# Layer one's last two token chunks of the first gMLP half as seven block products instead of eight

## The chip, the cores and the metric

One core of a Trainium2 chip. The time is the device time of one execution in microseconds (us). The engines are named as in the profile: PE (matrix products), PEld (its weight loads), DVE, ACT, POOL (vector, activation and GpSimd engines) and SP (the queue that issues most DMAs). Each engine runs its own queue in order and waits on semaphores for the others.

## What is computed

Two layers, each a linear-attention block and a gMLP block, on 2048 tokens of 512 features:

```python
x = x + A(layernorm(x))        # q, k, v; kv = pk^T v; o = pq kv / (pq . z); o @ wo
x = x + B(layernorm(x))
def B(x):
    z = gelu(x @ w_in)                     # (2048, 1792)
    z1, z2 = z[:, :896], layernorm(z[:, 896:])
    g = w_sp @ z2 + b_sp                   # mixing over the 2048 tokens
    return (z1 * g) @ w_out
```

The change concerns `z1`, the first half of `gelu(x @ w_in)`, in the first of the two layers (L = 0 in the code).

## The kernel before, in words

All products run on PE in fp32r parts: each operand is split into a high part (a rounded copy, made by ACT, `high`) and a low part (the rest, made by DVE, `low`), and a product is three matrix instructions (high by high, high by low, low by high).

Tokens are handled in 16 tiles of 128, and in four chunks of 512 (four tiles). For each layer there are three stages: `P1` (keys, queries, and the sum over keys), `P2` (attention output, second layer norm, and `x @ w_in`), and `P4` (mixing and `w_out`). `P2.run` is layer one's version of the second stage, a loop over steps s = 1 to 18. In step s it does, for different tiles:

- `b_high`, `b_low`: the queries of tile s, which went through DRAM to be turned, are turned back by DVE and split (ACT, then DVE);
- `c`, `c2`, `c3`: the attention output of tile s-1 on PE (12 instructions of 512 columns), added to x and its statistics taken on DVE, three small steps on POOL (`rs`, `rs`, `nb`), and the normalised tile (ACT) stored to DRAM in turned form (`yt`);
- `d_high`, `d_low`: tile s-2, back from DRAM, turned by DVE, split by ACT and DVE into its quarter of the chunk operand `xT`;
- `e`, `e2`, `e3`: tile s-3 times the second half of `w_in` (24 instructions of 448 columns), gelu on ACT, statistics on DVE, the three small steps on POOL; `e4`, one step later, normalises it on ACT;
- `f`: outputs of the first half, one (chunk, block of 128 features) each: 12 instructions of 512 columns, gelu (ACT), stored to DRAM. There are 4 chunks by 7 blocks. A chunk's seven become possible when its fourth tile is done (`d_low` with k == 3), and each step takes up to two.

`sums` are sums of blocks of `w_sp` for the seven-product mixing: a `tick` loads blocks, POOL makes two sums, and SP stores them two at a time. Layer one's P2 makes a tick in each step, and four are left (`LEFT`) for the first steps of its mixing. The five `f` that are left after step 18 run at the start of `P4.run`, while the first weights of the mixing are split (`sp`) and the first sums of z are made (`zahead`).

Layer two (`run2`, and the generator `tail`) already computes chunks 2 and 3 by seven products: the chunks are the two halves of the tokens, the features of x are halved, and the blocks f and f+3 of the weights are the two halves of the outputs. Three triples of weight sums (`FSums`) are made in layer two's `P1` on POOL and kept in DRAM (`w1sums`). `first_a` and `first_b` are products of chunk 2 alone; `T1`, `T2`, `raw` make sums of the token halves on DVE; `tail` has products 5, 6, 7, 3 and 4 for the three block pairs. A `yield` in it lets `P4.run` split the mixing's first weights in between. The seventh block (f = 6) is computed plainly.

The order on each engine is that of the code: nothing is reordered afterwards.

Of the kernel before, what the change touches and what calls it, by code (L numbers as in the profile page):

```python
# [152 lines left out]
def mixer_kernel(ctx: ExitStack, tc: tile.TileContext, x_in, wqkv, wo_d, win1_d, win2_d, wsp_d, bsp_d, wout_d,  # L153
# [299 lines left out]
    class P1:  # L453
# [187 lines left out]
        def run(self, sums):  # L641
            side = deque([self.win2] * NF)
            ND = NT - DEFER
            for s in range(1, NT + 2):
# [54 lines left out]
                if self.L:  # L699
                    if 9 <= s < NT + 1:  # L700
                        sums.halve(28 + (s - 9) // 2, None, (s - 9) % 2)
                    if s in WADD:
                        if not WADD[s]:
                            self.fsums = FSums()
                        self.fsums.load(WADD[s])
                    if s - 1 in WADD:
                        self.fsums.sums(WADD[s - 1])
                    if s - 2 in WADD:
                        self.fsums.split(WADD[s - 2])
                        if WADD[s - 2] == 2:  # L710
                            self.fsums.close()
# [15 lines left out]
    class FSums:  # L727


        def __init__(self):  # L730
            self.raw = quads.get([P, 2, 2, 512])
            self.parts = quads.get([P, 2, 2, 512], F32R)

        def load(self, f):
            for k in range(2):
                nc.sync.dma_start(self.raw[:, f % 2, k], win1_d[f + 3 * k])

        def sums(self, f):
            p, q = (self.raw[:, f % 2, k].rearrange("p (k n) -> p k n", k=2) for k in range(2))
            for o, a, b, op in ((q[:, 1], q[:, 0], q[:, 1], OP.add), (q[:, 0], p[:, 0], q[:, 0], OP.subtract),  # L740
                                (p[:, 0], q[:, 1], p[:, 0], OP.subtract), (p[:, 1], p[:, 1], p[:, 0], OP.subtract)):
                nc.gpsimd.tensor_tensor(o, a, b, op=op)

        def split(self, f):
            p, q = (self.raw[:, f % 2, k].rearrange("p (k n) -> p k n", k=2) for k in range(2))
            for m in range(2):
                h, l = (self.parts[:, m, k] for k in range(2))
                for k, s in enumerate((q[:, 1 - m], p[:, m])):
                    high(h[:, 256 * k:256 * k + 256], s)
                for k, s in enumerate((q[:, 1 - m], p[:, m])):  # L750
                    low(l[:, 256 * k:256 * k + 256], s, h[:, 256 * k:256 * k + 256])
                for k in range(2):
                    nc.sync.dma_start(w1sums[f, m][k], self.parts[:, m, k].bitcast(F32))

        def close(self):
            quads.put(self.raw, self.parts)
# [72 lines left out]
    class P2:  # L829
        def __init__(self, p1):  # L830
            self.L = L = p1.L
            self.p1 = p1
            self.win1, self.win2 = None if L else w_in1(), p1.win2
            self.ws = deque()
            self.wf = deque([w1parts[f] for f in list(range(NF)) * 2 + [0, 6, 1, 2, 6]]
                            + [w1sums[f, m] for m in range(2) for f in range(3)]
                            + [[t[:, 256:512] for t in w1parts[f + 3]] for f in range(3)])
            self.draw, self.S, self.fdone, self.qhome, self.zacc, self.meant = {}, {}, None, {}, {}, set()
            self.qturn, self.xturn = Turn(f"qt{L}", range(5), True), Turn(f"yt{L}", (0, 1, 2, 3, NT - 1) if L else range(4), home=ZHome if L else None)
# [44 lines left out]
        def b_high(self, i):  # L884
            b, home = self.qturn.get(i)
            self.qhome[i] = ZHome(i) if self.L and i > FIRSTPAIR else pages
            h = self.qhome[i].get([P, 4, P], F32R)
            high(h, b)
            self.bpart = b, home, h
# [23 lines left out]
        def c3(self, i):  # L913
# [3 lines left out]
            own = self.L and i > FIRSTPAIR  # L917
# [25 lines left out]
        def d_low(self, i):  # L943
# [9 lines left out]
            if k == 3:  # L953
                self.fnext = [(n, f) for f in (range(NF) if n < 2 or not self.L else (NF - 1,))]
# [149 lines left out]
        def f(self, hold=False, home=pages):  # L1104
# [19 lines left out]
            if f == NF - 1 and not (self.L and n > 1):  # L1124
                quads.put(*self.xT.pop(n))
# [38 lines left out]
        def first_a(self, *fs):  # L1164

            A = nc.scalar.activation
            for f in fs:
                w = self.A[f] = self.ws.popleft()
# [5 lines left out]
        def first_b(self, *fs):  # L1174

            for f in fs:
                w = self.A[f]
                self.fmul(self.u[f], [t[:, 256:512] for t in w], [t[:, 2:4] for t in self.xT[2]], False, True)
                pages.put(*w)

        def first_out(self, *fs):
            for f in fs:
                if f:
                    self.wfetch()
# [26 lines left out]
        def tail(self):  # L1211
            V, A = nc.vector, nc.scalar.activation
            h, l = (t.bitcast(F32) for t in self.xT[3])
            big = [bigs.get([P, NF, 512], F32R if k < 2 else F32) for k in range(3)]
            c = [big[2][:, f] for f in range(3)]
            room = Rooms(big[2][:, f] for f in range(3, NF))
# [11 lines left out]
            self.p4.loadb()  # L1228
# [10 lines left out]
            for f in range(3):  # L1239
# [4 lines left out]
                if f == 0:  # L1244
                    self.e3m(NT - 2)
                    self.e3m(NT - 1)
                if f == 1:
# [6 lines left out]
            self.e3(NT - 2)  # L1254
            self.e3(NT - 1)
            self.e4(NT - 4)
            self.e4(NT - 3)
# [19 lines left out]
            for i in (NT - 2, NT - 1):  # L1277
                _, rs, nb = self.zms.pop(i)
                V.tensor_scalar(ztile[i], ztile[i], rs, nb, op0=OP.mult, op1=OP.add)
            for f in range(3):  # L1280
                w = self.ws.popleft()
                self.fmul(d[f], w, self.T[4], False, True)
                pages.put(*w)
# [4 lines left out]
            bigs.put(*big)  # L1288

        def run(self, sums):  # L1290
# [4 lines left out]
            for s in range(1, NT + 3):  # L1295
                if s == NT + 2:
                    sums.tick()
# [17 lines left out]
                else:  # L1315
# [29 lines left out]
                self.f()  # L1345
                self.f()
# [4 lines left out]
                if self.L == 0:  # L1351
                    if s > 4:
                        sums.tick(s < NT + 2)
# [4 lines left out]
                if s >= NT + 1:  # L1358
                    self.p4.fetch(s - NT - 1)
# [270 lines left out]
    class P4:  # L1630
# [622 lines left out]
        def run(self, nxt):  # L2253
            p2 = self.p2
            early = nxt is None
            if not early:
                self.fetch(3)
                self.sp(0)
                self.fetch(4)
            self.zmade = 0  # L2260
            if not early:
                self.zahead(1)
            n = 0
            if early:
                for _ in p2.tail():
                    n += 1
                    self.zahead(n - 1)
                    self.sp(n - 1)
                    if n < 3:
                        self.fetch(n + 3)  # L2270
                self.zahead(3)
            while p2.f():
                self.zahead(min(self.zmade, 3))
# [3 lines left out]
                if n == SPN:  # L2277
                    self.sp(1)
                    self.fetch(5)
            self.zahead(3)  # L2280
            if p2.win1 is not None:
                p2.win1.free()
# [4 lines left out]
            for g in range(n):  # L2287
# [11 lines left out]
                if not early and g == 14:  # L2299
                    self.sums.fetch()  # L2300
                if not early and 15 <= g <= 15 + LEFT:
# [117 lines left out]
```

## Time and profile before

| | |
|---|---|
| median of 3 runs | 1346.38 us (1345.5 to 1346.66) |
| the profiled execution | 1345.32 us |
| its span, first to last instruction | 1343.5 us |
| busy share: PE, DVE, ACT, POOL | 100%, 78%, 54%, 34% |

Lists of groups have the line, engine, operation, tiles written and read, count, busy time, mean length of one, and the idle time before them with what ended it. A timeline has start and length in us first. A matrix instruction's length in the profile is longer than its share of PE, since they overlap: what one costs is the time from its start to the start of the next. Layer one's P2 lies at 133 to 331 us of the span, and its mixing starts at 350.3 us.

### The profile page before, as it was taken

The numbers are of one execution on the slowest core, as the hardware profiler recorded it, in microseconds if no ns is written. First come the engines' busy times: TensorE is split into PE (matmuls) and PEld (weight loads), VectorE is DVE, ScalarE is ACT, GpSimd is POOL, SyncE is SP. The second block draws the span as 40 slices with busy tenths as digits, with TensorE's granted clock in tenths as the row PEclk, the third lists the DMA queues.
The fourth block names the chain that finished last, engine by engine and source line by source line (L and its number), as shares of the span: only waits on it lengthen the run. The fifth ranks groups of instructions, "written<-read, shape, count | busy, mean of one in ns | idle before, by whom it ended". The sixth has DMA issues, their size and how long they took to land.

```text
span 1343.5 us, 19219 instructions
## 1 busy us (share of the span) xinstructions
PE 1338.9 (100%) x6547; PEld 1142.0 (85%) x6547; DVE 1042.9 (78%) x1662; ACT 726.6 (54%) x1219; POOL 460.2 (34%) x613
## 2 busy tenths in 40 slices
PE   9999999999999999999999999999999999999999
PEld 7888888888888888889988888888888888888898
DVE  7779877753797699898867878777679858899885
ACT  5764634334642265445677755557687433666454
POOL 3755765534122400301425443544531012122021
PEclk9999999999999999999999999999999999999999
DMA  5898477878977986894777662678767545579344
GB/s 184 284 313 282 158 256 250 284 254 270 316 234 256 289 267 203 282 320 80 174 169 235 167 142 84 202 243 259 229 211 234 170 164 176 178 245 312 123 79 64
DMA packets 172403, 290.30 MB, mean 216 GB/s; under 512 B 14480, under 2 KB 53904, under 8 KB 172048
## 3 DMA queue, kind: packets, MB, share of 16 engines
q1 hardware_dynamic: 154048, 251.45, 56.5%
q0 software_dynamic: 18112, 37.49, 13.4%
q8 instruction: 51, 0.84, 0.3%
q14 instruction: 48, 0.39, 0.1%
q10 hardware_dynamic: 144, 0.13, 0.0%
HBM read 204.08 MB, written 101.71 MB: 228 GB/s over the span
## 4 chain that ended last, share of the span: by engine, by line
PE 98%; DVE 1%; DMA 0%; ACT 0%; POOL 0%; issue 0%; SPq 0%; POOLq 0%
PE bank L230 14%; PE bank L228 14%; PE bank L229 14%; PE bank L1922 12%; PE bank L1923 12%; PE bank L1924 12%; PE bank L2120 3%; PE bank L2121 3%; PE bank L2122 3%; PE bank L988 1%; PE bank L989 1%; PE bank L990 1%; PE bank L384 1%; PE bank L1155 1%; PE bank L1157 1%; PE bank L1156 1%
## 5 line engine op out<-in xcount | busy, mean ns | idle before, releaser
L1923 PE MATMUL bank<-qd,pg 128*128 128x512 f32 x736 | 286.4, 389 | 0.0
L1922 PE MATMUL bank<-qd,pg 128*128 128x512 f32 x736 | 286.3, 389 | 0.0
L1924 PE MATMUL bank<-qd,pg 128*128 128x512 f32 x736 | 286.3, 389 | 0.0
L1697 ACT ACTIVATE qd<-qd 128x1024 fp32r<-128x1024 f32 x142 | 149.5, 1053 | 128.2 <-PE bank L1924 108.0
L1700 DVE TENSOR_TENSOR qd<-qd,qd 128x1024 fp32r<-128x1024 f32 x132 | 167.8, 1274 | 54.1 <-ACT qd L1697 54.1
L230 PE MATMUL bank<-qd,pg 128*128 128x512 f32 x448 | 174.7, 390 | 0.0
L1924 PEld LDWEIGHTS bank<-qd,pg 128*128 128x128 f32 x736 | 138.2, 188 | 28.8
L1923 PEld LDWEIGHTS bank<-qd,pg 128*128 128x128 f32 x736 | 138.2, 188 | 28.6
L1922 PEld LDWEIGHTS bank<-qd,pg 128*128 128x128 f32 x736 | 138.2, 188 | 28.6
L1963 POOL TENSOR_TENSOR bg<-bg,pg 128x512 f32<-128x512 f32 x28 | 46.9, 1676 | 217.9 <-ACT qd L1697 100.3
L228 PE MATMUL bank<-qd,pg 128*128 128x512 f32 x308 | 120.2, 390 | 0.2 <-ACT pg L214 0.2
L229 PE MATMUL bank<-qd,pg 128*128 128x512 f32 x308 | 120.0, 390 | 0.0
L230 PEld LDWEIGHTS bank<-qd,pg 128*128 128x128 f32 x448 | 84.1, 188 | 18.2 <-DVE pg L217 0.4
L363 POOL TENSOR_SCALAR rs<-mv 128x1 f32<-128x1 f32 x80 | 24.7, 308 | 191.3 <-DVE mv L361 186.9
L214 ACT ACTIVATE pg<-pg 128x512 fp32r<-128x512 f32 x85 | 53.0, 624 | 64.6 <-DVE pg L448 21.3
L372 ACT ACTIVATE pg<-pg,nb,rs 128x512 f32<-128x512 f32 x52 | 42.1, 812 | 84.5 <-POOL nb L366 79.0
L1606 POOL TENSOR_TENSOR pg<-pg,pg 128x512 f32<-128x512 f32 x48 | 67.2, 1400 | 58.2 <-DVE pg L1762 52.1
L2122 PE MATMUL bank<-wo,qd 128*128 128x256 f32 x288 | 81.5, 283 | 0.0
L2120 PE MATMUL bank<-wo,qd 128*128 128x256 f32 x276 | 78.1, 283 | 0.0
L2121 PE MATMUL bank<-wo,qd 128*128 128x256 f32 x276 | 78.0, 283 | 0.0
L229 PEld LDWEIGHTS bank<-qd,pg 128*128 128x128 f32 x308 | 57.8, 188 | 12.1 <-DVE qd L217 0.3
L228 PEld LDWEIGHTS bank<-qd,pg 128*128 128x128 f32 x308 | 57.8, 188 | 12.1 <-ACT pg L214 0.4
(278 smaller groups left out, 3280.4 us busy)
## 6 DMA issues: line engine op xcount, KB each, us to landing
qd<-s SPq DMA_DIRECT2D x62, 512.0 KB, 4.4
qd<-in_wsp_dram SPq DMA_DIRECT2D x40, 512.0 KB, 4.1
qd<-hP SPq DMA_DIRECT2D x40, 512.0 KB, 4.7
pg<-z SPq DMA_DIRECT2D x56, 256.0 KB, 4.7
pg<-in_wsp_dram SPq DMA_DIRECT2D x52, 256.0 KB, 4.3
s<-pg SPq DMA_DIRECT2D x48, 256.0 KB, 3.8
z<-pg SPq DMA_DIRECT2D x40, 256.0 KB, 3.3
pg<-w POOLq DMA_DIRECT2D x38, 256.0 KB, 4.7
```

The lines of the kernel that those rows point to most:

```text
L228: nc.tensor.matmul(out, ah, bh, start=start, stop=False)
L229: nc.tensor.matmul(out, ah, bl, start=False, stop=False)
L230: nc.tensor.matmul(out, al, bh, start=False, stop=stop)
L1606: nc.gpsimd.tensor_tensor(t, a, b, op=OP.add)
L1697: self.mark = nc.scalar.activation(w[:, 0], r, AF.Copy)
L1700: nc.vector.tensor_sub(w[:, 1], r, w[:, 0].bitcast(F32))
L1922: m(out, h[:, o], w[:, 0, j, :], start=start, stop=False, skip_group_check=True)
L1923: m(out, h[:, o], w[:, 1, j, :], start=False, stop=False, skip_group_check=True)
L1924: m(out, l[:, o], w[:, 0, j, :], start=False, stop=stop, skip_group_check=True)
L2120: m(out, A, x, start=start and f == 0, stop=False, skip_group_check=True)
L2121: m(out, A, y, start=False, stop=False, skip_group_check=True)
L2122: m(out, B, x, start=False, stop=stop and f == 2, skip_group_check=True)
```

## The change

Layer one's P2 takes chunks 2 and 3 by the same seven products. The tables that set the order are changed, `tail` serves both layers, and the weight sums are made in layer one's steps 13 to 16, on DVE and ACT, and stored for layer two. The shares of the first token half (`m = 0`) are kept in memory until `tail` uses them, those of `m = 1` are loaded again from DRAM in step 18. The split weights of layer one are stored to DRAM five steps earlier (`WSTORE`). Ticks of block sums stop after step 13, and ten instead of four are made in the mixing, from its 14th step on. Normalised tiles and query parts are held in the z tiles instead of pages (`ZHome`). Layer two's P1 no longer makes the weight sums.

```diff
-WSTORE = 9
+WSTORE = 4
+FONE = {6: 2, 7: 2, 8: 2, 9: 1, 10: 2, 11: 2, 12: 2, 13: 1, 14: 1}
-WADD = {2: 0, 4: 1, 6: 2}
+WADD = {13: 0, 14: 1, 15: 2}
-LEFT = 4
+LEFT = 10
+TLAST = 13
+TFIRST = 13
...
         def split(self, f):
+            raw = self.raw.pop(f)
+            p, q = (t.rearrange("p (k n) -> p k n", k=2) for t in raw)
+            V = nc.vector
+            V.tensor_add(q[:, 1], q[:, 0], q[:, 1])
+            V.tensor_sub(q[:, 0], p[:, 0], q[:, 0])
+            V.tensor_sub(p[:, 0], q[:, 1], p[:, 0])
+            V.tensor_sub(p[:, 1], p[:, 1], p[:, 0])
             for m in range(2):
...
-                self.fnext = [(n, f) for f in (range(NF) if n < 2 or not self.L else (NF - 1,))]
+                self.fnext = [(n, f) for f in (range(NF) if n < 2 else (NF - 1,))]
...
+                if s in (15, 16, 17):
+                    self.first_a(s - 15)
+                if s == NT + 1:
+                    self.T1()
+                    self.T1split()
+                    self.raw(1)
+                    self.T2()
+                if s == NT + 2:
+                    self.ws.extend(self.fsums.kept)
+                    quads.put(*self.xT.pop(2))
+                    for _ in range(3):
+                        self.wfetch()
                 if s >= 4:
                     self.e4(s - 4)
...
                     self.e3(s - 3)
-                self.f()
-                self.f()
+                for _ in range(FONE.get(s, 0)):
+                    self.f()
+                if s in (15, 16, 17):
+                    self.first_b(s - 15)
+                    self.first_out(s - 15)
+                if s - 2 in WADD:
+                    self.fsums.store()
+                if s in WADD:
...
+                    self.fsums.load(WADD[s])
+                if s - 1 in WADD:
+                    self.fsums.split(WADD[s - 1])
+                if s == NT:
+                    self.B = quads.get([P, 2, 2, 512])
+                    self.raw(0)
...
-            while p2.f():
-                self.zahead(min(self.zmade, 3))
+            for _ in p2.tail():
```

Three places of the built program, where the steps above the mixing stand. Tiles are named by pool (`pg` pages, `qd` quads, `bg` bigs, `z_z` a tile of the second half) and a running number.

DVE in step 16 and at the head of step 17 before the change: the add of tile 15's attention output to x with its statistics, the turning and low part of tile 14, the statistics of z13, then the turning of tile 15.

```order
L909 TENSOR_TENSOR pg_339_3238<-pg_339_3238,bank_131_3492 128x512
L359 BN_STATS st<-pg_339_3238 128x6
L361 BN_AGGR mv<-st 128x2
L448 STREAM_TRANSPOSE pg_362_3520<-pg_355_3405 128x4x128
L217 TENSOR_TENSOR qd_17_3279<-pg_362_3520,qd_16_3278 128x4x128
L359 BN_STATS st<-z_z_3553 128x6 x2
L361 BN_AGGR mv<-st 128x2
L448 STREAM_TRANSPOSE pg_367_3606<-pg_363_3525 128x4x128
L217 TENSOR_TENSOR qd_17_3279<-pg_367_3606,qd_16_3278 128x4x128
```

The same piece now, from the statistics of z13 on: four sums of a pair of weight blocks, four low parts, and `raw(0)` stand ahead of tile 15's turning.

```order
L362 BN_STATS st<-z_z_3558 128x6 x2
L364 BN_AGGR mv<-st 128x2
L733 TENSOR_TENSOR pg_330_3470<-pg_330_3470 128x256
L734 TENSOR_TENSOR pg_330_3470<-pg_329_3468,pg_330_3470 128x256
L735 TENSOR_TENSOR pg_329_3468<-pg_330_3470,pg_329_3468 128x256
L736 TENSOR_TENSOR pg_329_3468<-pg_329_3468 128x256
L220 TENSOR_TENSOR pg_338_3590<-pg_330_3470,pg_337_3589 128x256
L220 TENSOR_TENSOR pg_338_3590<-pg_329_3468,pg_337_3589 128x256
...
L1160 TENSOR_TENSOR qd_18_3601<-qd_14_2766,qd_15_2767 128x1024
L451 STREAM_TRANSPOSE z_y<-pg_335_3530 128x4x128
L220 TENSOR_TENSOR qd_17_3281<-z_y,qd_16_3280 128x4x128
```

Steps 14 and 15 have such a block of eight at their ends too, where they had none.

DVE from tile 15's low part to the first operand of product 6 now (before, only the two statistics of z14 and z15 stood there): `T1`, its low part, `raw(1)`, the eight of `T2`, the two statistics, and the low part of product 6's operand, `bg_7`.

```order
L220 TENSOR_TENSOR qd_17_3281<-z_y,qd_16_3280 128x4x128
L1194 TENSOR_TENSOR qd_18_3601<-qd_16_3280,qd_18_3601 128x1024
L1195 TENSOR_TENSOR qd_18_3601<-qd_18_3601,qd_17_3281 128x1024
L220 TENSOR_TENSOR qd_19_3618<-qd_18_3601,qd_19_3618 128x1024
L1160 TENSOR_TENSOR qd_18_3601<-qd_14_2766,qd_15_2767 128x1024
...
L1211 TENSOR_TENSOR pg_342_3623<-pg_342_3623,qd_17_3281 128x512
L362 BN_STATS st<-z_z_3661 128x6 x2
...
L362 BN_STATS st<-z_z_3727 128x6 x2
L364 BN_AGGR mv<-st 128x2
L220 TENSOR_TENSOR bg_7_3744<-pg_343_3624,bg_7_3744 128x512
```

ACT over the same stretch now: the high part of `T1`, then z13 normalised, gelu of z14, an output's gelu, z14 normalised, gelu of z15, z15 normalised, and only then the high part of product 6's operand.

```order
L217 ACTIVATE qd_19_3618<-qd_18_3601 128x1024
L375 ACTIVATE z_z_3558<-z_z_3558,nb,rs 128x896
L1068 ACTIVATE z_z_3661<-bank_137_3635 128x448
L1143 ACTIVATE pg_345_3680<-bank_136_3608 128x512
L375 ACTIVATE z_z_3661<-z_z_3661,nb,rs 128x896
L1068 ACTIVATE z_z_3727<-bank_139_3701 128x448
L375 ACTIVATE z_z_3727<-z_z_3727,nb,rs 128x896
L217 ACTIVATE bg_7_3744<-pg_343_3624 128x512
```

Before, the same rows for z13 to z15 stood there, but what followed them was the split of the mixing's first weight, not an operand that the next product reads.

More of the change, by code (lines that the diff above doesn't have):

```diff
@@ L730, in __init__ @@
         def __init__(self):
[L731 to L732 removed]
+            self.raw, self.kept, self.made = {}, deque(), []
         def load(self, f):
[L735 to L742, printed above, removed]
[L744 to L745 removed]
+            self.raw[f] = [load(win1_d[f + 3 * k]) for k in range(2)]
+        def split(self, f):
+            raw = self.raw.pop(f)
[5 more added lines that the diff above has]
+            V.tensor_sub(p[:, 1], p[:, 1], p[:, 0])
             for m in range(2):
[L747 removed]
+                h, l = pages.get(PAGE, F32R), pages.get(PAGE, F32R)
                 for k, s in enumerate((q[:, 1 - m], p[:, m])):
@@ L1123, in f @@
                 self.wfetch()
-            if f == NF - 1 and not (self.L and n > 1):
+            if f == NF - 1 and n < 2:
                 quads.put(*self.xT.pop(n))
@@ L1288, in tail @@
             bigs.put(*big)
+            if not L:
+                pages.put(*c)
         def run(self, sums):
```

118 lines of the change are left out of this document (58 added, 60 removed).

## The prediction

> **What bounds the kernel now.** I read the page first: busy shares, then the chain that ended last.
>
> ```profile
> span 1343.5 us, 19219 instructions
> PE 1338.9 (100%) x6547; PEld 1142.0 (85%) x6547; DVE 1042.9 (78%) x1662; ACT 726.6 (54%) x1219; POOL 460.2 (34%) x613
> PE 98%; DVE 1%; DMA 0%; ACT 0%; POOL 0%; issue 0%; SPq 0%; POOLq 0%
> ```
>
> PE is busy throughout and is 98% of the chain. A product that goes therefore shortens the span, and anything that makes PE wait lengthens it at once: there is no other slack to take it up. What a product costs, and how near the other engines are, I read from the busy time by stretches, cut at the first matrix instruction of a step: steps 13, 14, 17, 18, then the five last outputs `f`.
>
> ```profile
> 269.25:279.59 10.34, 10.34 (x50) 9.02 (x48) 6.63 (x14) 2.95 (x6) 4.36 (x7) 1.00 0.77 259
> 279.59:292.64 13.05, 13.05 (x61) 11.27 (x60) 7.71 (x11) 4.83 (x8) 5.31 (x10) 1.00 0.84 271
> 318.75:326.36 7.61, 7.61 (x37) 6.76 (x36) 1.78 (x2) 2.13 (x3) 3.37 (x4) 1.00 0.77 251
> 326.36:331.23 4.87, 4.87 (x26) 4.51 (x25) 1.36 (x3) 2.85 (x6) 2.39 (x5) 1.00 0.51 182
> 331.23:350.30 19.07, 19.07 (x86) 15.77 (x85) 8.73 (x17) 9.51 (x17) 7.39 (x8) 1.00 0.97 336
> ```
>
> The columns are length, then busy time of PE, PEld, DVE, ACT and POOL, clock, DMA share. The last stretch is seven outputs of 12 instructions: 19.07 / 84 = 0.227 us each. Step 13, with one output, takes 10.34; step 14, with two, 13.05.
>
> **What it removes.** Chunks 2 and 3 need 14 x 12 = 168 instructions now. After, the three block pairs need 3 x 7 x 6 = 126 and block 6 needs 24: 150. So 18 x 0.227 = **4.1 us** goes, the whole gain. On PE, steps 14, 15 and 16 become 10.34 long, so step 15 starts at 289.9, step 16 at 300.3, step 17 at 310.6, step 18 at 318.2 (before 326.36), if nothing waits. The rest of this part asks whether the others keep up.
>
> **Weight sums in steps 14 to 16.** The step loop is a relay of DVE, POOL and ACT, here step 15 of before, from the turning of query tile 15 to the statistics of z12:
>
> ```profile
> 298.81 1.10 DVE L448 STREAM_TRANSPOSE pg<-pg 128x512 f32<-128x512 f32 x1 [2.38 <-DMA pg<-qt]
> 301.22 0.68 DVE L909 TENSOR_TENSOR pg<-pg,bank 128x512 f32<-128x512 f32 x1
> 303.08 0.23 POOL L363 TENSOR_SCALAR rs<-mv 128x1 f32<-128x1 f32 x1 [2.63 <-DVE mv L361]
> 304.36 0.82 ACT L372 ACTIVATE pg<-pg,nb,rs 128x512 f32<-128x512 f32 x1 [3.78 <-POOL nb L366]
> 305.08 0.61 ACT L214 ACTIVATE qd<-pg 128x512 fp32r<-128x512 f32 x1
> 305.60 1.12 ACT L372 ACTIVATE z_z<-z_z,nb,rs 128x896 f32<-128x896 f32 x1
> 306.63 0.95 ACT L1070 ACTIVATE z_z<-bank 128x448 f32<-128x448 f32 x2
> 307.18 1.15 DVE L359 BATCH_NORM_STATS2 st<-z_z 128x6 f32<-128x448 f32 x2 [0.76 <-ACT z_z L1070]
> 308.43 0.21 DVE L361 BATCH_NORM_AGGREGATE mv<-st 128x2 f32<-128x12 f32 x1
> ```
>
> Every member waits for the one before, so DVE is held for 308.64 - 298.81 = 9.8 us, though busy for less. The weight sums come behind that in DVE's order and ahead of the next tile's turning. Their price is that of layer two's sums of the same width, and of ACT copies of 256 columns:
>
> ```profile
> 943.26 0.43 DVE L961 TENSOR_TENSOR z_y<-z_y 128x256 f32<-128x256 f32 x1
> 944.64 0.43 DVE L964 TENSOR_TENSOR z_y<-z_y 128x256 f32<-128x256 f32 x1
> L1805 ACT ACTIVATE pg<-z_z 128x256 fp32r<-128x256 f32 x60 | 21.2, 403 | 1.1 <-DMA z<-pg 1.1
> ```
>
> Four sums take 1.8. ACT's four high parts (0.36 from start to start) begin after the third, and the last low part ends some 1.5 behind the sums: 3.35 in all. So step 14 is 9.8 + 3.35 = 13.2, step 15 with one more ACT copy of a bank (0.5) 13.7, both against 10.34 on PE. Where does DVE start? Query tile 14 was turned here:
>
> ```profile
> 285.83 1.11 DVE L448 STREAM_TRANSPOSE pg<-pg 128x512 f32<-128x512 f32 x1 [1.26 <-DMA qt<-pg]
> 325.50 0.69 DVE L217 TENSOR_TENSOR qd<-pg,qd 128x512 fp32r<-128x512 f32 x1 [0.70 <-ACT qd L214]
> ```
>
> SP no longer stores weights in steps 11 to 13, so this comes earlier; not usefully before 282, as the product that is added next ends at 279.6 + 2.7. Bounds 282 and 285.8; I take 282, because two stores less in each of three steps outweigh the 3.8. Then 282 + 13.2 + 13.7 = 308.9 for the add of tile 15's output, which PE has had since 303.0. From there tile 14's high part is ready 4.5 on (301.22 to 305.69) at 313.4, while PE wants it at 310.6 + 1.4 = 312.0: **wait 1.4**. Step 16 on DVE is 308.64 - 301.22 = 7.4, the copy 0.5, the sums 3.35, `raw(0)` 1.15: tile 15 is turned at 321.3 and its low part starts 1.8 later, at 323.2. Step 18 on PE would now start at 319.6: **wait 3.6**. The second row above shows how bare this place is: in the kernel before the same low part ends at 326.19, 0.2 us ahead of step 18. What ticks on POOL and the DMAs gain here is small, since DVE, not the round trip through DRAM, comes last.
>
> **From tile 15 to product 6.** Layer two's trace has the same sums:
>
> ```profile
> 983.30 1.23 DVE L1193 TENSOR_TENSOR qd<-qd,qd 128x1024 f32<-128x1024 f32 x1
> 985.08 1.05 ACT L214 ACTIVATE qd<-qd 128x1024 fp32r<-128x1024 f32 x1
> 987.84 1.22 DVE L1162 TENSOR_TENSOR qd<-qd,qd 128x1024 f32<-128x1024 f32 x1
> 988.97 1.28 DVE L1204 TENSOR_TENSOR pg<-qd,qd 128x512 f32<-128x512 f32 x2
> 994.04 2.49 DVE L217 TENSOR_TENSOR bg<-pg,bg 128x512 fp32r<-128x512 f32 x4
> 976.93 2.17 POOL L205 DMA_DIRECT2D pg<-w1s  x4
> ```
>
> From the start of tile 15's low part: low 0.6, `T1` 2.5, its high 1.1, its low and `raw(1)` 2.3, the eight of `T2` 994.04 - 988.97 = 5.05: 11.55. Now DVE takes z14's statistics (1.46: 13.0), POOL its three steps (303.08 to 304.36, 1.3: 14.3), ACT z14's normalising and z15's gelu (305.60 to 307.18, 1.6: 15.9), DVE z15's statistics (17.4). On POOL the seven DMA issues of step 18 stand ahead of z15's steps, 7 x 0.54 = 3.8 behind 14.3 (18.1); without them 17.4 would hold. Three steps 1.3, normalising 1.05, high part 0.55, low part 0.7: **21.7**. PE has only z15's product 4.9, one output 2.7 and product 5 of 4.1 to do: 11.7. **Wait 10.0**, part of it ahead of product 5's last third, which needs a bank that z15's gelu frees. No such wait stands in layer two, where z14 and z15 are normalised behind product 6.
>
> So product 6 starts at 323.2 + 21.7 = 344.9, and 72 instructions later (16.35) the mixing, at 361.25 instead of 350.30: **+10.95**. The other way round: 1.4 + 3.6 + 10.0 - 4.1 = 10.9.
>
> **After a wait.** No row of before shows PE after a wait of microseconds, only its start from rest:
>
> ```profile
> 2.35 3.76 PE L619 MATMUL bank<-pg,ones 128*128 128x512 f32 x8
> ```
>
> Eight instructions in 3.76 instead of 1.8: 1.9 lost. Bounds 0 and 1.9 for each of three long waits; what two of them lose is hidden by the next wait. I take **1.9** once, since rest is the nearest case. The Trainium skill ("TensorE: Matmul & The Clock Gate", Part 1) says that PE falls to half its clock after an idle window of about 3.4 us and needs a busy one to recover; an estimate from it is 1.7 a spell, and the sum would be 0.2 lower. The trace's start agrees in kind.
>
> **Ticks in the mixing.** Six more ticks, 12 sums on POOL. They slow DVE:
>
> ```profile
> 393.58 6.96 POOL L1606 TENSOR_TENSOR pg<-pg,pg 128x512 f32<-128x512 f32 x4 [52.12 <-DVE pg L1762]
> 391.67 0.55 DVE L1737 TENSOR_TENSOR z_z<-z_z 128x384 f32<-128x384 f32 x1
> 394.47 1.65 DVE L1737 TENSOR_TENSOR z_z<-z_z 128x384 f32<-128x384 f32 x1
> ```
>
> A DVE subtraction beside a POOL sum takes 1.1 more. From the plain one's start to the slowed one's are 2.8 us, a mixing step's share of DVE without such sums; with two, 2.8 + 2 x 1.1 = 5.0. A step is 24 instructions, 5.45 on PE. It still fits: nothing, bounds 0 and 3. The Trainium skill ("SBUF — State Buffer", Who interferes with whom) has the rule that such a pair excludes each other for whole instructions, which speaks against moving ticks here; if each sum held DVE for its full 6.96 / 4 = 1.74, the step would be 2.8 + 2 x 1.74 = 6.3 and the sum up to 3 higher. The measured 1.1 decides. Weight stores in steps 4 to 10 load SP as steps 9 to 12 were loaded: nothing, at most 1. Layer two's P1 loses work that nobody waited for: nothing.
>
> **The sum.** From the profiled execution's 1345.32: + 10.95 + 1.9 = 1358.2. The median of the runs is 1.06 higher, so **1359**.
>
> **Rivals.**
> - *Only the wait ahead of product 6* (the weight sums fit because the DMAs are faster than I think): tile 15 in time for 318.2, product 6 at 339.9, mixing at 356.25: +6, and 0 to 1.9 for the clock: 1351 to 1354 on the median, 1348 if the round trip gives 2 and POOL's issues 0.8 more. Chance 0.22.
> - *The other side, no wait at all:* 1346.4 - 4.1 = 1342. It needs tile 15's low part 10 us ahead of step 18, so at 308. Its price is that of a round trip. In the kernel before tile 15 is normalised by ACT and turned by DVE at
>
> ```profile
> 314.03 0.81 ACT L372 ACTIVATE pg<-pg,nb,rs 128x512 f32<-128x512 f32 x1 [5.48 <-POOL nb L366]
> 323.71 1.09 DVE L448 STREAM_TRANSPOSE pg<-pg 128x512 f32<-128x512 f32 x1 [5.39 <-DMA pg<-yt]
> ```
>
>   so 323.71 - 314.03 = 9.7 lie between, and 304.36 - 301.22 = 3.1 from the add to ACT. The product of tile 15 ends at 303.0: 316 is the earliest, not 308. Chance 0.07.
> - *Half covered* (two more microseconds won in each of the terms above): 1344 to 1348, 0.07.
> - *More:* DVE starts step 14 at 285.8 (+3.8), a second slow spell (+1.9), mixing late (+3): 1362 to 1368. Chance 0.14.
> - That the change doesn't remove the products is excluded by the order of its instructions.
>
> The forecast, 1354 to 1362, has 0.50. The range 1348 to 1367 leaves the two faster cases and a little above. About 0.2% (2.7 us) is what a measurement can tell from no change: faster 0.07, the same 0.09, slower 0.84.
>
> **What would show it.** PE waiting for a DVE or ACT tile just ahead of product 6, in tile 15's step and a little in step 17; DVE late by some 6 us at tile 15's add; z15 normalised on ACT right ahead of product 6's operand; mixing at about 361; DVE nearly full but PE unbroken in the mixing's first plain steps; nothing moved in layer two but its P1's DMAs. I am wrong if product 6 follows product 5 without a wait, or if PE idles in the mixing.

## The result, and the profile after

The changed kernel takes 1362.49 us (median of 4 runs, 1361.44 to 1365.52), beside 1346.52 for the kernel before in the same comparison: a ratio of 1.0123, 95% interval 1.0105 to 1.0140. It is slower by 16.0 us. The profiled execution took 1361.44, with a span of 1359.7.

The page of the changed kernel has these lines for the span, the busy shares and the chain that ended last:

```profile
span 1359.7 us, 19248 instructions
PE 1341.1 (99%) x6529; PEld 1142.2 (84%) x6529; DVE 1074.7 (79%) x1700; ACT 735.1 (54%) x1234; POOL 464.2 (34%) x615
PE 94%; DVE 2%; DMA 1%; ACT 1%; POOL 0%; SPq 0%; issue 0%; DVEq 0%; ACTq 0%; POOLq 0%
```

PE has 6529 instructions instead of 6547: the 18 are gone. But PE is no longer the whole chain: 94% instead of 98%, and DVE, DMA and ACT stand in it. Busy time by stretches, cut at PE's steps: steps 14, 15, 16, 17 and 18, product 5, products 6 to 4, and the first 74 us of the mixing (length, then busy time and instructions of PE, PEld, DVE, ACT and POOL, the granted clock, the DMA share and GB/s):

```profile
279.30:289.63 10.33, 10.33 (x49) 9.02 (x48) 5.88 (x9) 4.34 (x7) 4.22 (x7) 1.00 0.73 222
289.63:309.14 19.51, 11.84 (x49) 9.84 (x48) 12.78 (x25) 9.51 (x17) 3.83 (x9) 0.87 0.77 242
309.14:320.22 11.08, 11.08 (x49) 9.59 (x48) 7.33 (x16) 5.67 (x11) 2.80 (x6) 0.93 0.70 235
320.22:328.59 8.37, 7.89 (x38) 6.68 (x36) 7.43 (x15) 3.17 (x7) 2.43 (x4) 1.00 0.84 310
328.59:336.20 7.61, 7.61 (x37) 6.76 (x36) 6.48 (x8) 3.44 (x5) 0.00 (x0) 1.00 0.20 53
336.20:347.84 11.64, 5.81 (x20) 3.89 (x18) 4.64 (x10) 3.70 (x6) 5.93 (x13) 0.73 0.67 209
347.84:366.21 18.37, 18.37 (x72) 14.77 (x73) 16.16 (x27) 15.15 (x27) 3.34 (x6) 0.90 0.56 182
366.21:440.00 73.79, 73.79 (x327) 61.12 (x326) 69.34 (x83) 34.29 (x49) 25.98 (x16) 1.00 0.87 294
```

Step 14 takes 10.33, as forecast. Step 15 takes 19.51, and PE is busy for 11.84 of it; product 5 takes 11.64 where its 18 instructions need 18 x 0.227 = 4.1. The mixing starts at 366.21 instead of 350.30, 15.9 later, and from there nothing more is lost: the same 327 instructions took as long before.

```profile
350.30:424.10 73.80, 73.80 (x327) 61.15 (x326) 64.85 (x84) 35.14 (x49) 13.66 (x8) 1.00 0.80 270
```

So all of it was lost between 290 and 366. The waits of PE there (who waits, for what, us in total, times, longest):

```profile
PE bank L1153 <- ACT bank L1170: 8.2, 2, 7.7
PE bank L1153 <- ACT z_z L1068: 3.5, 1, 3.5
PE bank L1153 <- ACT bg L217: 2.3, 1, 2.3
```

L1153 is the first instruction of each half-size product, L1170 is ACT's copy of the bank of `first_a`, which `first_b` goes on adding to. L1068 is the gelu of z15, whose bank product 5 wants next, and L217 on `bg` is the high part of product 6's operand.

The timeline of DVE, from the turning of query tile 14 to tile 15's low part (start and length first):

```profile
285.81 1.10 DVE L451 STREAM_TRANSPOSE pg<-pg 128x512 f32<-128x512 f32 x1 [1.55 <-DMA pg<-qt]
299.04 1.07 DVE L451 STREAM_TRANSPOSE pg<-pg 128x512 f32<-128x512 f32 x1
301.42 0.68 DVE L907 TENSOR_TENSOR pg<-pg,bank 128x512 f32<-128x512 f32 x1
312.83 0.69 DVE L907 TENSOR_TENSOR pg<-pg,bank 128x512 f32<-128x512 f32 x1 [0.46 <-PE bank L233]
324.83 1.08 DVE L451 STREAM_TRANSPOSE z_y<-pg 128x512 f32<-128x512 f32 x1
326.61 0.69 DVE L220 TENSOR_TENSOR qd<-z_y,qd 128x512 fp32r<-128x512 f32 x1 [0.70 <-ACT qd L217]
```

Tile 14's add stands at 301.42, where it stood before (301.22), though PE is 3.0 earlier into step 15 (289.63 instead of 292.64). The relay did not follow PE. Where PE shows this is on ACT, in step 15:

```profile
304.55 0.81 ACT L375 ACTIVATE z_y<-pg,nb,rs 128x512 f32<-128x512 f32 x1 [3.77 <-POOL nb L369]
305.79 0.58 ACT L1170 ACTIVATE bank<-bank 128x512 f32<-128x512 f32 x1
346.13 1.13 ACT L375 ACTIVATE z_z<-z_z,nb,rs 128x896 f32<-128x896 f32 x1 [3.13 <-POOL nb L369]
347.17 2.17 ACT L217 ACTIVATE bg<-pg 128x512 fp32r<-128x512 f32 x4
```

The copy, whose bank was done long before, stands behind the normalising of tile 14, which waits for tile 14's add. The last two rows are the place ahead of product 6: z15 is normalised, and right behind it comes the operand.

### The profile page after: what moved, and what is told of

Its sections match the earlier page's. It is cut to its first block, busy times and chain, and to the rows that moved or that the text cites. A ratio compares the mean times of both kernels' runs of the same rounds, so it can differ in the third digit from the quotient of the medians.

```text
span 1359.7 us, 19248 instructions
## 1 busy us (share of the span) xinstructions
PE 1341.1 (99%) x6529; PEld 1142.2 (84%) x6529; DVE 1074.7 (79%) x1700; ACT 735.1 (54%) x1234; POOL 464.2 (34%) x615
## 4 chain that ended last, share of the span: by engine, by line
PE 94%; DVE 2%; DMA 1%; ACT 1%; POOL 0%; SPq 0%; issue 0%; DVEq 0%; ACTq 0%; POOLq 0%
PE bank L1965 12%; PE bank L1964 12%; PE bank L1963 12%; PE bank L231 12%; PE bank L233 12%; PE bank L232 12%; PE bank L2161 3%; PE bank L2162 3%; PE bank L2163 3%; PE bank L1153 1%; PE bank L986 1%; PE bank L988 1%; PE bank L987 1%; PE bank L1154 1%; PE bank L1155 1%; DMA yt<-z_y 1%
## 5 line engine op out<-in xcount | busy, mean ns | idle before, releaser
L1963 PE MATMUL bank<-qd,pg 128*128 128x512 f32 x736 | 286.3, 389 | 0.0
L1964 PE MATMUL bank<-qd,pg 128*128 128x512 f32 x736 | 286.3, 389 | 0.0
L1965 PE MATMUL bank<-qd,pg 128*128 128x512 f32 x736 | 286.3, 389 | 0.0
L233 PE MATMUL bank<-qd,pg 128*128 128x512 f32 x448 | 174.9, 391 | 0.0
L1964 PEld LDWEIGHTS bank<-qd,pg 128*128 128x128 f32 x736 | 138.2, 188 | 28.8
L1963 PEld LDWEIGHTS bank<-qd,pg 128*128 128x128 f32 x736 | 138.2, 188 | 28.7
L1965 PEld LDWEIGHTS bank<-qd,pg 128*128 128x128 f32 x736 | 138.2, 188 | 28.3
L231 PE MATMUL bank<-qd,pg 128*128 128x512 f32 x264 | 103.3, 391 | 0.2 <-ACT pg L217 0.2
L232 PE MATMUL bank<-qd,pg 128*128 128x512 f32 x264 | 102.9, 390 | 0.0
L233 PEld LDWEIGHTS bank<-qd,pg 128*128 128x128 f32 x448 | 84.3, 188 | 18.3 <-DVE pg L220 0.4
L1647 POOL TENSOR_TENSOR pg<-pg,pg 128x512 f32<-128x512 f32 x48 | 70.2, 1463 | 58.2 <-DMA pg<-in_wsp_dram 56.1
L217 ACT ACTIVATE pg<-pg 128x512 fp32r<-128x512 f32 (+1 forms) x86 | 50.3, 593 | 42.5 <-DVE pg L1832 19.0
L545 POOL TENSOR_TENSOR pg<-pg,pg 128x512 f32<-128x512 f32 x30 | 39.9, 1331 | 57.2 <-DVE pg L539 55.4
L231 PE MATMUL bank<-bg,qd 128*128 128x448 f32 x160 | 59.0, 369 | 0.0
L231 PEld LDWEIGHTS bank<-qd,pg 128*128 128x128 f32 x264 | 49.6, 188 | 11.0 <-DVE pg L220 0.7
```

Of the source, the lines that this page charges most:

```text
L231: nc.tensor.matmul(out, ah, bh, start=start, stop=False)
L232: nc.tensor.matmul(out, ah, bl, start=False, stop=False)
L233: nc.tensor.matmul(out, al, bh, start=False, stop=stop)
L1647: nc.gpsimd.tensor_tensor(t, a, b, op=OP.add)
L1963: m(out, h[:, o], w[:, 0, j, :], start=start, stop=False, skip_group_check=True)
L1964: m(out, h[:, o], w[:, 1, j, :], start=False, stop=False, skip_group_check=True)
```

## The experiments

Three questions: does the copy make PE wait, or the relay behind it; what are the weight sums worth; and what holds product 6. Every ratio is to the kernel before, timed on the same chip; the changed kernel's is 1.0123. Diffs are cut, with `...` where lines are left out.

**The copy ahead of the normalising.**

```diff
                     self.a2_mul(s + 2)
+                    if s in (15, 16):
+                        self.first_a(s - 15)
...
-                if s in (15, 16, 17):
+                if s == NT + 1:
                     self.first_a(s - 15)
```

> The first half-products of chunk 2 in steps 15 and 16 are issued right behind the attention output, so ACT's copy of their bank stands ahead of the normalising of tile 14 (15). In the changed kernel PE waited 7.84 us at 298.4 for that copy. Relay theory (the chain DVE-POOL-ACT of steps 14 to 16 is what is late, the copy only decides where PE shows it): that wait goes but comes back ahead of the w_in products of tiles 13 to 15; tile 15's low part moves from 326.6 to 325 at best (three copies of 0.5 out of the relay); 1 to 3 us faster than the changed kernel, 1359 to 1361. Copy theory (only the copy's place in ACT's order makes PE wait): 7.8 and the slow spell behind it go, 1352 to 1354, and tile 15's low part comes some 8 earlier.

Measured: 1360.91, ratio 1.0112 (1.0097 to 1.0127), not to be told from the changed kernel. Its waits of PE:

```profile
PE bank L1153 <- ACT bank L1170: 6.4, 2, 3.8
PE bank L1153 <- ACT bg L217: 3.6, 1, 3.6
PE bank L1153 <- ACT z_z L1068: 2.0, 1, 2.0
```

7.7 in one piece became 2.6 in step 15 and 3.8 in step 17, and tile 15's low part starts at 326.02 instead of 326.61. The copy theory is out. The copy now stands behind the high part of query tile 15, whose turning stands behind the weight sums.

**z14 and z15 normalised behind product 6.**

```diff
-                if s >= 4:
+                if 4 <= s < NT + 2:
                     self.e4(s - 4)
...
-                    self.e3(s - 3)
+                    if s < NT + 1:
+                        self.e3(s - 3)
...
             split(*self.T[4], b21)
+            if not L:
+                for i in (NT - 2, NT - 1):
+                    self.e3(i)
+                for i in (NT - 2, NT - 1):
+                    self.e4(i)
...
-            self.e4(NT - 1)
             self.win2.free()
```

> Statistics and normalising of z14 and z15 stand behind product 6 instead of ahead of its operand; nothing else differs. Order theory: product 5's last third and product 6 wait together 0 to 1 instead of 7.7, the slow spell behind (2) goes too: 7 to 10 faster, 1352 to 1355; the 7.84 in step 15 stays. Rival (the eight sums of T1, raw and T2 on DVE, 11.5 us behind tile 15's low part, set product 6): 0 to 3 faster. Second rival: the mixing's first sums of z now wait for z14 and z15 instead, and half of the gain is given back there.

Measured: 1357.86, ratio 1.0088 (1.0071 to 1.0104), 3 us above order theory's range. Stretches of product 5, products 6 to 4, and the mixing's first 73.8 us:

```profile
337.16:341.24 4.08, 4.08 (x19) 3.38 (x18) 4.04 (x7) 2.27 (x5) 1.01 (x2) 1.00 1.12 406
341.24:357.56 16.32, 16.32 (x73) 13.51 (x72) 12.24 (x23) 10.03 (x17) 3.70 (x9) 1.00 0.46 150
357.56:431.36 73.80, 71.08 (x304) 57.84 (x303) 68.74 (x85) 37.51 (x55) 24.34 (x19) 0.98 0.85 290
```

Order theory holds up to the mixing: product 5 takes its 4.08, and products 6 to 4 take 16.32 instead of 18.37. The mixing starts at 357.56, 8.65 earlier. But in as many us it now does 304 instructions instead of 327, which is 23 x 0.227 = 5.2 given back. The second rival was right on the amount, but not on the way: PE waits there for splits of weights (`qd`, 1.7 and 1.0), not for sums of z. ACT makes these splits behind the normalising of z14, for which it stands idle, and behind a wait for a store that frees a page:

```profile
351.13 1.14 ACT L375 ACTIVATE z_z<-z_z,nb,rs 128x896 f32<-128x896 f32 x1 [4.01 <-POOL nb L369]
368.23 0.63 ACT L217 ACTIVATE pg<-pg 128x512 fp32r<-128x512 f32 x1 [3.48 <-DMA z<-pg]
```

**The same, in the gap behind product 6's operands.** The statistics stand ahead of the copies for product 6, where DVE waits for ACT; ACT normalises between those copies.

```diff
             pages.put(*self.t2, *self.b22)
+            if not L:
+                for i in (NT - 2, NT - 1):
+                    self.e3(i)
...
                 V.tensor_add(y, y, c[f])
+                if not L and f < 2:
+                    self.e4(NT - 2 + f)
```

> Like the late normalising, but the statistics of z14 and z15 stand right behind the splits of product 6's and 7's operands, and ACT normalises them between its copies for product 6, about 5 us earlier than there. Order theory: product 6 follows product 5 without a wait, as in the late normalising, and the 3.3 us that PE then lost in the mixing's first steps (waiting for sums of z that need z14 and z15) go: 3 to 4 faster than the late normalising, 1353 to 1355. Rival (those waits come from the weights' splits of the mixing, which stand later on ACT and DVE in any case): the same as the late normalising, 1357 to 1358.

Measured: 1353.27, ratio 1.0048 (1.0033 to 1.0063), as order theory had it. The mixing starts at 356.84 and loses nothing:

```profile
356.84:430.64 73.80, 73.80 (x327) 61.15 (x326) 69.79 (x84) 34.84 (x50) 26.01 (x16) 1.00 0.87 293
```

ACT waits for a page here too (3.2 us at 363.3, 6.5 behind the mixing's start), but PE does not. So about 9 of the 16.0 us were the place of z14 and z15 in two queues. The wait in step 15 stayed at 7.7.

**Weight sums in earlier steps.** `WADD = {9: 0, 10: 1, 11: 2}`, all six pairs stored and loaded again in step 17. (With three pairs kept in memory, as in the changed kernel, sums in steps 10 to 12 do not fit, as no page is left for them; so there is no time for `e2_sums_early` and, with both other edits, `e4_all`.)

> The weight sums are made in steps 10 to 12 instead of 14 to 16, all six pairs are stored and loaded again (three more pairs of loads in step 17). Relay theory: DVE is 3.0 earlier at tile 14's add (301.4 to about 298), the wait of 7.84 becomes 4 to 5, tile 15's low part comes 2.4 to 3.4 earlier (its trip through DRAM stays), the wait ahead of product 6 stays at 7 to 8: 2.5 to 5 faster, 1357 to 1360. Rival (DVE waits for DRAM in these steps anyway and the sums lie in that wait): within 1 us of the changed kernel. Second rival: steps 10 to 12 take on the wait, since DVE there is 9.2 busy of 13.25 already.

Measured: 1375.86, ratio 1.0217 (1.0201 to 1.0232), 13 us slower than the changed kernel. The second rival came true, for a reason that none had named. DVE at the low parts of the first sums:

```profile
253.10 0.76 DVE L220 TENSOR_TENSOR pg<-pg,pg 128x256 fp32r<-128x256 f32 x2 [4.48 <-DMA x<-pg]
257.40 0.76 DVE L220 TENSOR_TENSOR pg<-pg,pg 128x256 fp32r<-128x256 f32 x2 [3.54 <-issue]
```

The first low parts wait 4.5 us for a store that frees a page, and DVE's queue stands behind them; what the next ones wait for the trace does not name. This says that there was no room for the sums in steps 10 to 12, not what the sums cost. Two kernels with these early sums and both other edits tell the same, and say nothing more of the relay:

> Sums in steps 10 to 12, the copy ahead of the normalising, and z14 and z15 normalised in the gap. Relay and order theory: tile 15's low part at about 321, PE waits 1 to 3 in steps 15 to 18 together and 0 to 1 ahead of product 6: 1343 to 1347, about the kernel before. If relay is not the cause, the wait of some 8 in steps 15 to 18 stays: 1350 or more.

Measured: 1364.88, ratio 1.0131 (1.0115 to 1.0148).

> As the one before, but the sums in steps 8, 10 and 12, so that no two steps in a row carry them on DVE. If sums in three steps in a row push DVE late into step 13, this is 1 to 3 faster than that one: 1342 to 1344. If DVE has room in steps 10 to 12, both are the same within 0.5.

Measured: 1359.06, ratio 1.0088 (1.0071 to 1.0104). DVE waits 10.5 us there for the stores of the sums.

**The sums left out.**

```diff
-            V.tensor_add(q[:, 1], q[:, 0], q[:, 1])
...
-                    high(h[:, 256 * k:256 * k + 256], s)
...
+                for k, t in enumerate((h, l)):
+                    nc.sync.dma_start(t.bitcast(F32), w1parts[f][k])
```

> The four sums of a block pair and their split on ACT and DVE are left out in steps 14 to 16; the pages are filled from the stored split weights by SP instead, so the products of chunks 2 and 3 use weights that are not the sums. Relay theory: DVE turns query tile 15 at about 296 instead of 299.0, adds tile 14 at 298.2 instead of 301.4, the wait of 7.84 becomes 4 to 5, tile 15's low part comes 3 to 4 earlier; the wait ahead of product 6 stays. 3 to 5 faster, 1357.5 to 1359.5. Rival (the sums fill DVE's own waits and cost nothing): within 1 of the changed kernel.

Measured: 1366.72, ratio 1.0154 (1.0136 to 1.0173), slower, against both theories. Its waits of PE for the copies, the turning of tile 15 on DVE, and tile 15's store on SP:

```profile
PE bank L1147 <- ACT bank L1164: 9.5, 2, 4.8
```

```profile
329.87 1.08 DVE L451 STREAM_TRANSPOSE z_y<-pg 128x512 f32<-128x512 f32 x1 [7.12 <-DMA pg<-yt]
```

```profile
321.02 0.60 SPq L422 DMA_DIRECT2D yt<-z_y  x1
```

The wait in step 15 fell from 7.7 to 4.8, but not because the copy came sooner. PE goes on at the same time as in the changed kernel, here the first row:

```profile
306.41 0.79 PE L1153 MATMUL bank<-qd,bg 128*128 128x512 f32 x1 [7.67 <-ACT bank L1170]
306.59 0.79 PE L1147 MATMUL bank<-qd,bg 128*128 128x512 f32 x1 [4.84 <-ACT bank L1164]
```

It is PE that reaches this product 3.0 later, 1.3 of it by a wait at 284.6 for tile 11's high part. The relay did get shorter: from the turning of query tile 14 to that of query tile 15 are 10.8 us (288.36 to 299.19) instead of 13.2. But it started 2.55 later. A new wait of 4.6 stands in step 17: the four loads that take the place of the sums stand ahead of tile 15's store on SP, and DVE waits 7.1 for that tile. So the sums cost this piece of the relay 2.4 us; what PE would win without them is not shown, since SP's queue is a part of the relay and this edit lengthened it.

**The sums in DVE's own waits.** The four sums between a tile's turning and its low part, the low parts a step later ahead of the z statistics.

```diff
                         self.d_high(s - 2)
+                        if s - 1 in WADD:
+                            self.fsums.split(WADD[s - 1])
                         self.d_low(s - 2)
...
                     self.e2(s - 3)
+                    if s - 2 in WADD and s <= NT:
+                        self.fsums.lows()
                     self.e3(s - 3)
```

> The same sums in the same steps, but the four sums stand between a tile's turning and its low part, where DVE waits 1.8 us for ACT, and the four low parts a step later ahead of a z tile's statistics, where DVE waits 1.3 for the gelu. Relay theory: 3 us of DVE a step go into its own waits, so this is within 1 us of the kernel without the sums: 1358 to 1360. Rival (their place does not matter, DVE is simply full): as the changed kernel, 1361 to 1363.

Measured: 1362.54, ratio 1.0127 (1.0109 to 1.0145): as the rival had it. Together with the copy and the normalising in the gap:

> The sums in DVE's waits, the copy of the first half-products ahead of the normalising, and z14 and z15 normalised in the gap behind product 6's operands. Relay and order theory: the wait of 7.84 shrinks to 0 to 2, PE waits 1 to 3 for tile 15, 0 to 1 ahead of product 6: 1343.5 to 1347. If the three reasons are all of it and tile 15 comes in time: 1342, faster than before by the 18 instructions.

Measured: 1354.43, ratio 1.0062 (1.0046 to 1.0078), no better than the normalising alone. What DVE waits for in the first of the two:

```profile
DVE pg L733 <- DMA pg<-in_win_dram: 5.1, 3, 2.0
```

The sums stood in a wait, but then waited themselves: their weight blocks are the last loads that SP issues in a step, and the earlier place was too early for them. In the first kernel's trace PE goes on with the product in step 15 at 305.24, 1.2 earlier, but has waited 1.7 for tile 12's low part, which now stands behind the sums.

**The turned queries loaded earlier.**

```diff
                 self.loadx(s + 1)
-                self.qturn.load(s + 1)
+                if s < 13 or s > 14:
+                    self.qturn.load(s + 1)
...
                 self.xturn.load(s - 1)
+                if s in (12, 13):
+                    self.qturn.load(s + 2)
```

> Only the place of two loads on SP's queue is changed: the turned queries of tiles 14 and 15 are loaded right behind the loads of the normalised tiles in steps 12 and 13, ahead of the outputs, block sums and weight blocks of those steps. In the changed kernel DVE turned query tile 14 at 285.8, set free by that load. Start theory (the relay of steps 14 to 16 is late because DVE starts it at 285.8, when this load has landed, and each tile after it inherits that): tile 14 is turned about 3 earlier, at 282 to 283, tile 14's add at about 298, the wait of 7.84 becomes 4 to 5, and the kernel is 2.5 to 4.5 faster: 1358 to 1360. Rival (sums, ACT or the trip of the normalised tile set the relay's pace, whenever it starts): within 1 of the changed kernel.

Measured: 1361.81, ratio 1.0121 (1.0104 to 1.0138): the rival. Query tile 14 is turned without a wait, but the next turning now waits for tile 12's trip through DRAM:

```profile
284.81 1.05 DVE L451 STREAM_TRANSPOSE pg<-pg 128x512 f32<-128x512 f32 x1
291.36 1.09 DVE L451 STREAM_TRANSPOSE z_y<-pg 128x512 f32<-128x512 f32 x1 [1.72 <-DMA pg<-yt]
299.02 1.07 DVE L451 STREAM_TRANSPOSE pg<-pg 128x512 f32<-128x512 f32 x1
```

With the query there, the normalised tile's own trip comes last, and query tile 15 is turned at 299.02 as ever.

**All together**, with the weight blocks loaded by POOL at the head of a step (`nc.gpsimd.dma_start(t, win1_d[f + 3 * k])`), the early query loads, the sums in DVE's waits, the copy ahead, and z14 and z15 in the gap:

> The sums in DVE's waits with their weight blocks loaded by POOL at the head of a step (in the kernel of that kind before, DVE waited 2.1 to 3.6 for those loads, issued late by SP), the early query loads, the copy ahead of the normalising, z14 and z15 normalised in the gap. Start theory with order theory: the wait in step 15 is 0 to 2, tile 15's low part comes at 319 to 322 and PE waits 1 to 3 for it, 0 to 1 ahead of product 6: 1343 to 1347. If the start of the relay does not matter: as the kernel of that kind before less the loads' wait, 1350 to 1353.

Measured: 1349.48, ratio 1.0029 (1.0018 to 1.0039), 2.5 above the expected range. It is 3.9 us slower than the kernel before in its own comparison, where the changed kernel was 16.0: 12 us are back, and the first wait is gone. All waits of PE over 0.2 us in steps 15 to 18 and the tail:

```profile
PE bank L1164 <- ACT bank L1181: 2.6, 1, 2.6
PE bank L233 <- DVE qd L220: 0.9, 1, 0.9
PE bank L1164 <- ACT bank L1273: 0.4, 1, 0.4
```

Step 15 runs without a break. The wait of 0.9 is for tile 14's low part, that of 2.6 for the copy that stands behind tile 15's high part.

**Nothing ahead of tile 15.** On top of that, tile 15's add and turning stand ahead of the low parts of the sums, `raw(0)`, and the statistics of z12 and z13; z13 goes behind product 6.

```diff
                         self.d_high(s - 2)
+                        if s == NT + 1:
+                            self.fsums.lows()
...
+                        self.fsums.lows()
+                        self.e3(NT - 4)
                     self.a2_mul(s + 2)
...
-                if 4 <= s < NT + 2:
+                if 4 <= s < NT + 1:
                     self.e4(s - 4)
```

> The kernel with all edits before, and on DVE's queue nothing that can wait stands ahead of tile 15 any more: its add comes ahead of the low parts of the first weight sums and the statistics of z12, its turning ahead of raw(0), the later low parts and the statistics of z13, which moves behind product 6's operands; the first stores of weight sums stand behind tile 15's store on SP. In the kernel before it, tile 15 was added at 307.9, 3.5 after its product, and PE waited 2.7 and 1.1 in step 17 and lost some 1.5 to a slow clock behind it. Relay theory (what stands ahead of tile 15 in DVE's and SP's order makes PE wait): tile 15's add at 305 to 306, its low part 2 to 3 earlier, at 319 to 320, the waits of step 17 fall to 0 to 1: 3 to 5 faster, 1344.5 to 1346.5, level with the kernel of before. Rival (the trip through DRAM, some 8 us behind the normalising, sets it whatever stands ahead): within 1 of the kernel with all edits, 1348.5 to 1350.5.

Measured: 1351.34, ratio 1.0052 (1.0038 to 1.0066). Waits of PE, and the mixing's first 73.8 us:

```profile
PE bank L1164 <- ACT bank L1278: 1.6, 1, 1.6
PE bank L1999 <- ACT qd L1774: 1.5, 1, 1.5
PE bank L2000 <- DVE qd L1777: 0.8, 1, 0.8
PE bank L1164 <- ACT bank L1181: 0.4, 1, 0.4
```

```profile
350.83:424.63 73.80, 71.51 (x307) 58.26 (x306) 68.57 (x85) 37.10 (x55) 21.96 (x16) 0.98 0.88 289
```

The time is above the ranges of both theories. Relay theory was right on tile 15: its low part starts at 318.6, 3.1 earlier than with the edits before, and the wait of 2.6 in step 17 is gone; the 0.4 for a copy is one in step 15. The mixing starts at 350.83, half a microsecond after that of the kernel before. But 20 of its instructions are late (307 instead of 327, 4.5 us). The rows name splits of weights (`qd`) again. On ACT they stand behind the normalising of z13, for which ACT now idles 3.3 us (345.42), and behind a wait of 3.3 for a store that frees a page (361.02, 10.2 behind the mixing's start). The kernel with all edits before has such a wait too, only 6.9 behind that start, and PE lost nothing there. So z13's new place is the likely reason; it was not tried apart. No version beat the kernel before.

## Why the prediction came out as it did

The sign was right, and so was the wait ahead of product 6 with its reason; the first wait stood elsewhere than forecast. The size was 3.2 us short of the profiled execution (1358.2 against 1361.44) and 3.5 of the median (1359 against 1362.49), just above the likeliest range of 1354 to 1362. By its own terms:

| term | forecast | measured |
|---|---|---|
| instructions gone | 18, 4.1 us | 18 |
| DVE turns query tile 14 | 282 (bounds 282 and 285.8) | 285.81 |
| from there to query tile 15 | 13.2 | 13.2 |
| from there to tile 15's add | 13.7 | 13.8 |
| tile 15's add to its turning | 12.4 | 12.0 |
| tile 15's low part starts | 323.2 | 326.6 |
| from there to product 6 | 21.7 | 21.2 |
| product 6 to the mixing | 16.35 + 1.9 | 18.4 |
| ticks in the mixing | nothing | nothing |
| mixing starts | 361.25 + 1.9 | 366.21 |

**The step that was mis-sized** is "I take 282, because two stores less in each of three steps outweigh the 3.8". It came at the other bound, 3.8 later, and everything behind inherited that. This is the first term of the rival *More* (chance 0.14), whose 1362 to 1368 holds the median; its other two terms added nothing. Before and after, the load of the query on SP, and after it the row ahead of the query's turning on DVE:

```profile
279.70 0.68 SPq L196 DMA_DIRECT2D pg<-qt  x1
279.94 0.59 SPq L199 DMA_DIRECT2D pg<-qt  x1
284.06 0.21 DVE L364 BATCH_NORM_AGGREGATE mv<-st 128x2 f32<-128x12 f32 x1
```

The two weight stores are gone from SP, but SP's load of tile 12 had to wait for that tile's store and was issued at 276.09 instead of 274.36, so the query's load, behind it in the queue, came no earlier. And DVE was busy with the statistics of z10 until 284.3 (284.6 before), so 282 was out of reach in this order of work. The early query loads show the same: issued 2.8 earlier, the query was turned at 284.81, right behind these statistics; then the trip of tile 12 through DRAM is next, and DVE is no earlier at query tile 15.

Of the 13.8 to tile 15's add the last 0.46 is a wait for PE: the forecast had that product done at 303.0, but with the wait in step 15 it came near 312.8.

**A wait was seen at the wrong place.** The forecast had 1.4 in step 17 and 3.6 in step 18, and took ACT's copy of a bank as 0.5 us of the relay. PE waited 7.7 for that copy in step 15 instead. Moving the copy moved the wait and left the time unchanged within its interval, so the copy decides where PE shows the relay's lag and not how large it is.

**The wait ahead of product 6** was forecast at 10.0; product 5 took 11.64 where 4.1 were needed, so 7.6 (5.8 of waits, the rest at a granted clock of 0.73). The reason given (z14 and z15 in the queues ahead of the operand) is shown by their move: the 7.6 went to nothing. Measured from tile 15's low part, product 6 came as forecast; the wait is smaller because PE itself was later, `first_b(2)` having to wait for its copy behind tile 15 too.

**Weight sums.** They hold DVE for 3.0 us ahead of query tile 15 (296.03 to 299.04; 3.35 was forecast), and without them that piece of the relay is 2.4 shorter. What they cost PE isn't shown: leaving them out loaded SP, moving them forward met full pages, and only with their loads on POOL did the move into DVE's waits stand in a kernel that gained on the normalising alone, among other edits. So the part of the 16 us that is not the place of z14 and z15 is shown for the edits together and not for any one of them. **Ticks** cost nothing: DVE was busy 69.3 instead of 64.9 of the mixing's first 73.8, and PE ran unbroken.

Still open is what keeps the fully edited kernel 0.29% slower than before. Its span is 3.7 us longer, and PE waits 6.2 in its trace from 275 on, 2.1 more than the 18 instructions save. Beside the waits shown, these are 1.4 at 283.4 for tile 11's high part and 0.9 in the mixing, near 470; neither has a cause shown, and they weren't tried apart.

## What to carry to other kernels

Where a few engines hand a tile around, making PE's share shorter moves nothing until the relay is shorter too: look for the time at which the relay reaches a tile, not only at how busy its engines are, and where two bounds of that time lie far apart, ask what would be late next before taking the early one. A sum that is put "into a wait" must have its operands there by then, and each queue that it passes through (SP's loads, pages, ACT's copies) is a part of the relay. Work that is moved behind an urgent operand has a reader of its own: z14 and z15 were free in one place and cost 5 us some 7 us later.

## What the runs showed of the hardware

The granted clock was 0.87 in the stretch with PE's wait of 7.7 and 0.93 behind it, and 0.90 behind the waits ahead of product 6, where some 2 us were lost as forecast. It is not the length of a wait alone that decides. With the copy ahead, a wait of 2.6 left 0.71:

```profile
302.29:308.12 5.83, 5.83 (x18) 4.63 (x19) 3.37 (x6) 2.60 (x4) 1.06 (x3) 0.71 0.84 257
```

With all edits together, another of 2.6, in step 17, left the clock whole in as many us behind it:

```profile
322.18:328.01 5.83, 5.83 (x28) 5.28 (x29) 4.67 (x5) 3.22 (x5) 0.00 (x0) 1.00 0.38 147
```

The Trainium skill ("TensorE: Matmul & The Clock Gate", Part 1) puts the fall to half clock behind an idle window of about 3.4 us; both of these waits were shorter, and behind the first the clock fell all the same, so here the measurement decides.
